# One decode step over a K and V cache: the rows of each 8 MB chunk stored in another order, and the copies' source pattern changed to match

## The chip, the cores and the metric

The kernel runs on one core of one Trainium2 chip. The metric is the device time of one execution in microseconds. The core has a matrix engine (PE, with its weight loads shown as PEld), a vector engine (DVE), a scalar engine (ACT), GpSimd (POOL) and a queue processor (SP) that here does nothing but issue transfers. Sixteen DMA engines move the data between the chip's main memory (HBM) and the core's on-chip memory (SBUF, 128 partitions).

## The reference

One token goes through one transformer block. Its attention part has 32 query heads over 8 K/V heads, with a cache of 65,536 positions of 128 numbers for each K/V head, in fp32:

```python
Hq, Hkv, Sk, Dh = 32, 8, 65536, 128
q = (x @ wq).reshape(B, Sq, Hq, Dh).transpose(0, 2, 1, 3)
k = jnp.repeat(k_cache, rep, axis=1)
v = jnp.repeat(v_cache, rep, axis=1)
scores = jnp.einsum("bhqd,bhkd->bhqk", q, k) * (Dh ** -0.5)
p = _softmax(scores, axis=-1)
o = jnp.einsum("bhqk,bhkd->bhqd", p, v)
...
h = x + _A_ref(_layernorm(x, axis=-1), A_k_cache, A_v_cache, A_wq, A_wo)
h2 = h + _B_ref(_layernorm(h, axis=-1), B_w_gate, B_w_up, B_w_down)
```

`_B_ref` is a gated feed-forward part of width 1792 with no nonlinearity: `((x @ w_gate) * (x @ w_up)) @ w_down`. There is one query row, so every number of the two caches is used once for each of four query heads, and the caches are nearly all of the data: 2 x 8 x 65,536 x 128 x 4 bytes = 536.9 MB.

## The kernel before, in words

The host cuts the K cache and the V cache of each of the 8 heads into 4 chunks. A chunk is 16,384 positions, laid out as 128 rows of 16,384 fp32 numbers, that is 128 rows of 64 KB, 8.39 MB together. For each head the 4 K chunks come first and the 4 V chunks after them, so there are 64 chunks, stored one after the other in one HBM tensor `kvd` (line 500 on). Row p of a chunk goes to partition p of the on-chip buffer.

There are two such buffers, `kv[0]` and `kv[1]` (line 62), each of the size of a chunk. SP issues the transfers of all large inputs in one order. First comes the query weight `wq` into `kv[1]` (line 118). Then the chunks follow, the even ones into `kv[0]` by `even` (line 113) and the odd ones into `kv[1]` by `odd` (line 116). Each is one copy of 128 rows. Behind the chunks come the output weight `wo`, the gate and up weights `gu` and the down weight `wd`, cut into pieces along the columns (line 149). Before each chunk but the first, SP waits for one count of the semaphore `free` (lines 139 to 144, the wait itself is in the helper `take`, line 104): that count is given when PE has finished reading the buffer into which the next transfer goes. So up to two transfers are on their way at a time, and the next one is issued when a buffer has been used.

PE reads a chunk in 32 windows of 512 columns (`windows`, line 353; the trace shows 64 matmuls per chunk; each has 32 columns of weights, and four in a row use the four quarters of the columns of the array). It waits for the chunk's semaphore before the first window (line 350): the semaphore counts 16 per copy, so all rows of a copy must have landed. For a K chunk the result is the scores of 16,384 positions, which ACT copies out of PSUM (line 217) and DVE reduces to a maximum (line 239). After four K chunks the maximum is joined over the partitions (lines 402 to 404), ACT makes the exponentials (line 221), PE transposes them (line 409), DVE writes them into the weight tile `st` (line 258), and the V chunks are multiplied by them. DVE adds the partial results (lines 269 to 274).

After the last head the output projection, the second layer norm and the feed-forward part run on the pieces of `wo`, `gu` and `wd`, and a 48 KB result goes out (line 477).

The change touches only the lines 113 and 116 and the host's expression for `kv` at line 504. The matmuls, the waits, the semaphores, the order of the issues and the content of the buffers `kv[0]` and `kv[1]` after a copy are the same.

Of the kernel before, what the change touches and what calls it, by code (L numbers as in the profile page):

```python
# [8 lines left out]
P = 128  # L9
D = 512  # L10
HKV, REP, DH = 8, 4, 128
SK = 65536
CK = 16384
NT = SK // CK
# [27 lines left out]
def body(nc, xr, kvd, wq, wo, gu, wd, out):  # L42
    pe_e, dve_e, act_e, pool_e, sp = nc.tensor, nc.vector, nc.scalar, nc.gpsimd, nc.sync

    def tile(name, *shape, align=32):
        return nc.alloc_sbuf_tensor(name, list(shape), F32, align_bytes=align).ap()
# [15 lines left out]
    kv = [tile(f"kv{i}", P, CK, align=1024) for i in range(2)]  # L62
# [22 lines left out]
    def sem(name):  # L85
        sems.append(nc.alloc_semaphore(name))
        return sems[-1]
# [7 lines left out]
    s_a0, s_a4, s_a24 = (sem(f"s_a{i}") for i in (0, 4, 24))  # L95
    s_b0, s_b20, s_b28 = (sem(f"s_b{i}") for i in (0, 20, 28))
# [13 lines left out]
        take(dve_e, own)  # L110

    def even(g):
        sp.dma_start(kv[0], kvd[g]).then_inc(s_a0, 16)

    def odd(g):
        sp.dma_start(kv[1], kvd[g]).then_inc(s_b0, 16)

    sp.dma_start(kv[1], wq).then_inc(s_b0, 16)
    pe_e.br("pe_main")
# [16 lines left out]
    pool_e.br("fin")  # L136

    even(0)
    with nc.Fori(1, end - 1, 2, engines=SP_ONLY) as c:
        for i, put in enumerate((odd, even)):  # L140
            take(sp, free)
            put(c + i)
    take(sp, free)
    odd(end - 1)

    def pieces(cuts, shift, buf, src, marks):
# [371 lines left out]
```

## Time and profile before

| | |
|---|---|
| median of 3 runs | 1308.97 us (1308.73 to 1309.02) |
| profiled execution, its own time | 1308.38 us |
| span of that execution in the trace | 1307.1 us |
| busy: PE, PEld, DVE, ACT, POOL | 676.0, 189.1, 101.6, 54.9, 4.7 us |
| moved by DMA in the span | 564.71 MB, 432 GB/s |
| time of the packets on the large queue | 99.8% of 16 engines' span |

The span runs from the first to the last instruction. Busy times leave out the issuing of transfers, branches and semaphores. A packet is one piece of a transfer as one DMA engine moves it; for a chunk a packet is one 64 KB row. The view of the transfers in a window splits the window into 40 equal slices and credits a packet's bytes to the slice in which it ends. "DMA to landing" is the time from a transfer's issue to its last byte. In the lists of groups the columns are line, engine, operation, output and input tiles, shapes, count, then busy time and mean duration, then idle time ahead of the group and what ended it.

### The profile page before, as it was taken

Reading aid. Unit: us, or ns where it says so; the run is one execution under the profiler, and the core shown is the slowest. Engines: PE = TensorE matmul, PEld = TensorE weight load, DVE = VectorE, ACT = ScalarE, POOL = GpSimd, SP = SyncE. Lnnn points to the kernel's source line nnn. Section 1 sums busy time; section 2 is a strip of 40 time slices with the busy share of each in tenths; the row PEclk is TensorE's granted clock in tenths of the full one; section 3 lists DMA queues with packets and bytes.
Section 4 is the critical chain, followed back from the end, with each engine's and each line's share of the span. In section 5 each row is a group of like instructions: output and inputs, shape, how many; then the busy total and the mean of one; then the engine's idle time right before and its main releaser. Section 6 shows DMA issues by size and latency. Waiting matters only on the chain. (4 is left out here: it accounts for less than half of the span.)

```text
span 1307.1 us, 10762 instructions
## 1 busy us (share of the span) xinstructions
PE 676.0 (52%) x4600; PEld 189.1 (14%) x4600; DVE 101.6 (8%) x250; ACT 54.9 (4%) x106; POOL 4.7 (0%) x14
## 2 busy tenths in 40 slices
PE   3446445445535545554643654454564455456458
PEld 0101111111101111111110211111111111111112
DVE  1001010010001000000100101001000100000011
ACT  0000000000000000000000000000000000000000
POOL 1000000000000000000000000000000000000000
PEclk9677677678777767767767776766776776786779
DMA  9999999999999999999999999999999999999999
GB/s 417 423 443 427 439 439 427 441 425 449 417 449 417 449 417 449 417 449 417 449 429 437 439 427 449 417 449 417 449 417 449 417 449 417 449 423 443 435 420 382
DMA packets 11154, 564.71 MB, mean 432 GB/s; under 512 B 1249, under 2 KB 1297, under 8 KB 1810
## 3 DMA queue, kind: packets, MB, share of 16 engines
q1 hardware_dynamic: 11152, 564.71, 99.8%
q10 hardware_dynamic: 2, 0.00, 0.0%
HBM read 564.66 MB, written 0.05 MB: 432 GB/s over the span
## 5 line engine op out<-in xcount | busy, mean ns | idle before, releaser
L353 PE MATMUL ps<-kv,st 128*32 128x512 f32 x4304 | 614.2, 734 | 562.7 <-DMA kv<-in_kv 542.9
L353 PEld LDWEIGHTS ps<-kv,st 128*32 128x32 f32 x4304 | 148.6, 132 | 1013.0 <-DMA kv<-in_kv 587.3
L239 DVE TENSOR_REDUCE mx<-sc 128x1 f32<-128x512 f32 x32 | 21.9, 686 | 578.9 <-DVEq L104 578.9
L409 PE MATMUL ptp<-ident,ex 128*128 128x128 f32 x128 | 28.2, 383 | 19.8 <-ACT ex L221 19.5
L217 ACT COPY sc<-ps 128x512 f32<-128x512 f32 x32 | 18.8, 586 | 438.3 <-ACTq L104 438.2
L221 ACT ACTIVATE ex<-sc,nbias 128x512 f32<-128x512 f32 x32 | 22.9, 715 | 305.9 <-ACTq L104 305.9
L271 DVE TENSOR_TENSOR orow<-ps,orow 128x512 f32<-128x512 f32 x16 | 11.1, 692 | 262.6 <-DVEq L104 262.6
L217 ACT ACT_TABLE_LOAD x8 | 10.3, 1283 | 429.0 <-ACTq L104 429.0
L258 DVE COPY st<-ptp 128x512 f32<-128x512 f32 x32 | 22.1, 692 | 45.3 <-DVEq L104 45.3
L409 PEld LDWEIGHTS ptp<-ident,ex 128*128 128x128 f32 x128 | 21.4, 196 | 22.4 <-ACT ex L221 22.3
L402 PE MATMUL sm<-ident,m 128*1 128x128 f32 x16 | 4.6, 289 | 28.3 <-DVE m L241 18.7
L274 DVE TENSOR_TENSOR orow<-ps,orow 128x256 f32<-128x256 f32 x16 | 6.1, 420 | 136.8 <-DVEq L104 136.8
L269 DVE COPY orow<-ps 128x512 f32<-128x512 f32 x8 | 5.5, 692 | 98.5 <-DVEq L104 98.5
L404 PE MATMUL sm<-ones,mexp 1*128 1x1 f32 x32 | 6.9, 281 | 6.8 <-DVE mexp L248 6.8
L440 PE MATMUL ptp<-ident,orow 128*128 128x128 f32 x32 | 6.6, 293 | 3.0 <-DVE orow L274 3.0
L402 PEld LDWEIGHTS sm<-ident,m 128*1 128x1 f32 x16 | 1.3, 79 | 42.9 <-DVE m L241 26.0
L404 PEld LDWEIGHTS sm<-ones,mexp 1*128 1x128 f32 x32 | 5.5, 213 | 9.5 <-DVE mexp L248 8.6
L221 ACT ACTIVATION_READ_ACCUMULATOR ex<-sc,nbias 128x1 f32 x32 | 6.0, 188 | 0.0
L231 DVE COPY st<-qx 128x1024 f32<-128x1024 f32 x8 | 5.6, 694 | 1.2
L373 PE MATMUL junk<-sc,mean_m 128*128 128x512 f32 x10 | 5.1, 619 | 0.0
L345 PE MATMUL ps<-ident,xn_row 1*128 1x1 f32 x4 | 0.6, 246 | 7.5 <-DVE xn_row L176 7.5
L201 DVE COPY gu_sb<-ps 128x256 f32<-128x256 f32 x4 | 1.5, 420 | 33.9 <-DVEq L104 33.9
(80 smaller groups left out, 62.9 us busy)
## 6 DMA issues: line engine op xcount, KB each, us to landing
kv<-in_wo SPq DMA_DIRECT2D x1, 5120.0 KB, 23.5
kv<-in_gu SPq DMA_DIRECT2D x1, 4096.0 KB, 20.2
kv<-in_wo SPq DMA_DIRECT2D x1, 2048.0 KB, 27.9
kv<-in_gu SPq DMA_DIRECT2D x1, 2048.0 KB, 24.6
kv<-in_wd SPq DMA_DIRECT2D x2, 1024.0 KB, 16.0
kv<-in_kv SPq DMA_DIRECT2D x64, 29.1
kv<-in_wo SPq DMA_DIRECT2D x1, 1024.0 KB, 11.8
kv<-in_gu SPq DMA_DIRECT2D x1, 1024.0 KB, 26.6
```

The source lines that it names most:

```text
L217: act_e.copy(sc[s], ps[s % 2]).then_inc(ad, 1)
L221: act_e.activation(ex[s - n], sc[s], AF.Exp, bias=nbias[:, 0:1], scale=SCALE, accum_out=sums[:, s:s + 1]).then_inc(atok[s - n], 1)
L231: dve_e.tensor_copy(st, qx.rearrange("p (g c) -> p g c", c=32)).then_inc(qt, 2)
L239: dve_e.tensor_reduce(out=mx[:, s:s + 1], in_=sc[s], axis=AX.X, op=ALU.max).then_inc(own, 1)
L258: dve_e.tensor_copy(st[:, :, 0:16].rearrange("p g (b h) -> p b g h", h=REP), ptp[n % 2].rearrange("p (b g h) -> p b g h", b=4, h=REP)).the ...
L271: mine(dve_e.tensor_tensor(out=orow, in0=ps[n % 2], in1=orow, op=ALU.add))
L274: dve_e.tensor_tensor(out=orow[:, cs], in0=ps[1][:, cs], in1=orow[:, cs], op=ALU.add).then_inc(tob, 1)
L353: i = mm(ps[buf][32 * j:32 * j + 32, :], st[:, 8 * j + r, :], kv[buf][:, w * 512:(w + 1) * 512], start=(r == 0), stop=(r in (1, 7)), skip_ ...
L402: pe_e.transpose(sm[1][0:1, 0:P], m1, ident).then_inc(pd, 1)
L404: mm(sm[0][:, 0:1], mexp.rearrange("p g h -> p (g h)"), ones[0:1, 0:1], start=True, stop=True).then_inc(pd, 1)
L409: i = pe_e.transpose(ptp[half][:, b * P:(b + 1) * P], ex[half][:, b * P:(b + 1) * P], ident)
L440: i = pe_e.transpose(ptp[1][:, b * P:(b + 1) * P], orow[:, b * P:(b + 1) * P], ident)
```

## The change

The host stores the 128 rows of each chunk in another order. The rows are seen as 16 groups of 8 (old row 8e + s, e from 0 to 15, s from 0 to 7), and are stored as 8 groups of 16, so that new row 16s + e holds old row 8e + s. The copy's source pattern undoes this: it walks e outermost (16 steps of one row, 64 KB), then s (8 steps of 16 rows, 1 MB), then the 16,384 numbers of the row. The destination pattern is unchanged: 128 partitions, one row each. So partition 8e + s receives the same numbers as before, from another address.

```diff
     def even(g):
-        sp.dma_start(kv[0], kvd[g]).then_inc(s_a0, 16)
+        sp.dma_start(kv[0], kvd[g].rearrange("(s e) x -> e s x", e=16)).then_inc(s_a0, 16)
 
     def odd(g):
-        sp.dma_start(kv[1], kvd[g]).then_inc(s_b0, 16)
+        sp.dma_start(kv[1], kvd[g].rearrange("(s e) x -> e s x", e=16)).then_inc(s_b0, 16)
...
         "kv": np.concatenate([
             lay(A_k_cache, HKV, NT, P, TPC, DH, perm=(0, 1, 4, 3, 2)).reshape(HKV, NT, P, CK),
             lay(A_v_cache, HKV, NT, P, CK),
-        ], axis=1).reshape(2 * HKV * NT, P, CK),
+        ], axis=1).reshape(2 * HKV * NT, 16, 8, CK).transpose(0, 2, 1, 3).reshape(2 * HKV * NT, P, CK),
```

The transfers of `wq`, `wo`, `gu`, `wd`, of the input row and of the result are not touched.

## The prediction

> **What bounds the kernel now.** I read the page from the top: span, busy shares, transfers.
>
> ```profile
> span 1307.1 us, 10762 instructions
> ## 1 busy us (share of the span) xinstructions
> PE 676.0 (52%) x4600; PEld 189.1 (14%) x4600; DVE 101.6 (8%) x250; ACT 54.9 (4%) x106; POOL 4.7 (0%) x14
> ...
> DMA packets 11154, 564.71 MB, mean 432 GB/s; under 512 B 1249, under 2 KB 1297, under 8 KB 1810
> ## 3 DMA queue, kind: packets, MB, share of 16 engines
> q1 hardware_dynamic: 11152, 564.71, 99.8%
> ...
> L353 PE MATMUL ps<-kv,st 128*32 128x512 f32 x4304 | 614.2, 734 | 562.7 <-DMA kv<-in_kv 542.9
> ```
>
> No compute engine is busy for more than 52% of the span, while the packets of the large queue fill 99.8% of what sixteen DMA engines have. PE's main group stands idle for 562.7 us, 542.9 of them waiting for chunks. The kernel is bound by its transfers from end to end.
>
> How even is that stream? Next I read the groups of the two lines that issue chunks, for the spacing of the issues, and the windows by stretch.
>
> ```profile
> L113 SPq DMA_DIRECT2D kv<-in_kv x32: 332/333/422, 1.2 to 1210.1; - x32
> ...
> DMA to landing us min/median/max: 28.2/29.1/40.8
> ```
>
> ```profile
> L116 SPq DMA_DIRECT2D kv<-in_kv x32: 332/333/343, 32.1 to 1229.9; - x32
> ```
>
> ```profile
> core 0: us, PE busy (x) PEld busy (x) DVE busy (x) ACT busy (x) POOL busy (x), PEclk, DMA share, GB/s
> 0.00:20.00 20.00, 0.58 (x4) 0.50 (x4) 4.56 (x16) 1.58 (x2) 4.68 (x14) 1.00 1.00 420
> 20.00:40.00 20.00, 11.73 (x76) 3.68 (x76) 1.95 (x6) 0.00 (x0) 0.00 (x0) 0.92 0.97 419
> 100.00:1200.00 1100.00, 568.43 (x3855) 158.51 (x3855) 82.19 (x189) 48.81 (x96) 0.00 (x0) 0.73 1.00 434
> ```
>
> The 32 issues of the odd chunks lie between 32.1 and 1229.9 us, so 31 intervals of two chunks take 1197.8 us, or **19.32 us per chunk**. A chunk is 128 rows of 65,536 bytes, so this is 434.2 GB/s, the 434 of the long window. If each engine takes 8 of the 128 rows, a row takes 19.32 / 8 = **2.415 us** and one engine moves 27.1 GB/s. A transfer lands 29.1 us after its issue (median) though its own moving takes 19.32, so it waits 9.8 us behind its predecessor; the queue is never empty.
>
> The last view is the one that I rest the forecast on: the transfers between 600 and 620 us, in slices of 0.5 us.
>
> ```profile
> DMA  0009000690009900099000990009600090006900
> GB/s 0 0 0 2097 0 0 0 262 1835 0 0 0 786 1311 0 0 0 1180 918 0 0 0 1442 655 0 0 0 1835 262 0 0 0 2097 0 0 0 262 1835 0 0
> DMA packets 144, 8.39 MB, mean 419 GB/s; under 512 B 16, under 2 KB 16, under 8 KB 16
> ```
>
> A slice at 2097 GB/s holds 1.05 MB, which is 16 rows. Rows end in bursts of 16, within one slice or two neighbouring ones, and then nothing ends for about 2 us. So **the sixteen engines go in step**, all at the same 27.1 GB/s, and they still do so after thirty chunks: neither the compute beside them nor the chunk makes one of them late. Had HBM been the limit I would expect engines to get ahead of one another; a rate this rigid looks like a fixed limit that each engine meets alone.
>
> **The change, part by part.** It adds and removes no instruction; a chunk stays 128 rows of 64 KB. What moves is which address each row has, and which engine carries which row to which partitions.
>
> (a) *Issue.* The source pattern has one more dimension. An issue takes 333 ns now; the slowest copy that SP issues, 422 ns, bounds what a longer pattern might add by 0.1 us, and I allow as much again. Below nothing it can't matter either: the 9.8 us that a transfer waits behind its predecessor hide it. Without that cover it would be 64 x 0.1 = 6 us. I take 0.
>
> (b) *Reading neighbours.* The gain that it could bring is bounded by the rows. In the steady stretch a row takes 2.415 us whatever else happens. The poorest stretches are the first two windows, 420 and 419 GB/s against 434. All of the shortfall there is (434 - 419.5) / 434 x 40 us = 1.3 us, and only the part after `wq` has changed addresses. I take 0, with -1.3 as the end on this side. For a loss through the reading order the nearest row is the same: 3.3% slower over the whole stream is 0.033 x 1236 = +41 us.
>
> (c) *Writing.* This is where I choose. The source's outermost dimension becomes 16, the destination's stays 128 partitions. If a copy is dealt out by outermost index, engine e now gets source group e. By the order in which both patterns are walked that is partitions 8e to 8e + 7, one after another. Before, both sides counted 128, and the trace doesn't show which 8 partitions one engine had. Suppose that data enters SBUF through sixteen entrances, each serving a fixed group of partitions at no more than the 27.1 GB/s that one engine moves. Today's even rate then says that today's deal puts one engine on each entrance. A deal in neighbouring eights need not. If two engines in step write to one entrance and half of the entrances stand idle meanwhile, each row takes two row times, 4.83 us. They don't part again by themselves, since the burst view shows that engines keep step. The ends are 0 (a deal that collides nowhere) and one more row time per row (every row collides with one other): 64 chunks x 8 rows x 2.415 us = **+1236.5 us**. I take the upper end, less what the engines' small stagger saves. A pair that is apart by t collides t less in each half of a chunk. The bursts lie within one or two slices, so t is 0.5 us at most, and the pair that is closest together sets the landing; with 0.1 us it is 128 x 0.1 = 13 us.
>
> [...] The trace agrees with sixteen engines per copy: 78 copies on the large queue make 1248 of the 1249 packets under 512 B. [...]
>
> (d) *What is late next.* PE waits longer: a chunk then comes each 38.6 us, and PE's idle time grows by about the 1236 us. A buffer is free again some 10 us after its chunk landed, as now, and the next issue still falls into the transfer of the other buffer, so the queue stays full. The tail is unchanged:
>
> ```profile
> 1283.89 17.78 DMA kv<-in_wd
> ```
>
> **The sum.** The profiled execution took 1308.4 us (span 1307.1 and 1.3 around it), 0.6 under the median of 1309.0. 1308.4 + 1236.5 - 13 = **2532 us**.
>
> **The rivals.**
>
> *Nothing changes* (the other side). The limit of 27.1 GB/s sits in the DMA engine itself, or the rows go to the engines as before, so that the change doesn't do what it says or does it without effect. For it: the rigid rate, which an engine's own limit explains as well; reading order can't matter to such an engine. Against it: it needs a place without an entrance limit, or a deal that doesn't collide. It decides as soon as no two engines share an entrance in the same row time. Time: 1308.4 + 0 to + 2, say 1309 us.
>
> [...]
>
> *Rows are read more slowly.* One engine's successive rows now lie 1 MB apart rather than 64 KB. If the reading of rows at that distance, by engines that keep step, meets in the same part of HBM, each per cent longer row costs 0.01 x 1236.5 = 12.4 us. With the nearest row's 3.3% it is 1350 us. For it: the engines' common step. Against: at any moment the sixteen engines would read one stretch of 1 MB. [...] No run here shows a large pitch.
>
> *Faster.* Neighbouring rows help the first chunks and shave the row time. The 1.3 us of (b) are within noise; a gain over 0.2% needs rows under 2.41 us in the whole stream: 1305 us.
>
> **How the numbers follow.** Collisions in step 55%, out of step 16%, slower reading 6%, nothing 20%, faster 3%. So slower by over 0.2% has 77%, within 0.2% (2.6 us, about what a measurement of this kernel can tell from no change) 20%, faster 3%. The likeliest time is 2532 us, its own range 2480 to 2550. The cases below it can't be left out, since leaving out no change and faster alone would be 23%; so the range is 1307 to 2560, and 3% (faster) and a few per cent above remain outside.
>
> **What would show it.** Right: the issues of line 116 are 77 us apart instead of 38.6, the long window shows 217 GB/s while the queue's share of packets stays near 100%, bursts of 16 rows come 4.83 us apart, and from the `wo` pieces on the rate is back at about 430. Out of step: rows of two lengths, bursts broken up. Slower reading: all rows longer by one ratio that isn't two. Wrong: an issue spacing of 38.6 us and unchanged bursts. Then (c) failed, and the limit was the engines' own or the deal didn't collide.

## The result, and the profile after

The changed kernel takes 2659.9 us (median of 6 runs, 2655.9 to 2669.2) against 1308.9 us before: a ratio of **2.034, 95% interval 2.031 to 2.036**. The profiled execution has a span of 2667.8 us.

The page of the changed kernel, in the same order as for the kernel before:

```profile
span 2667.8 us, 10762 instructions
## 1 busy us (share of the span) xinstructions
PE 678.2 (25%) x4600; PEld 189.6 (7%) x4600; DVE 103.0 (4%) x250; ACT 54.9 (2%) x106; POOL 4.4 (0%) x14
...
DMA packets 11154, 564.71 MB, mean 212 GB/s; under 512 B 1249, under 2 KB 1297, under 8 KB 1810
## 3 DMA queue, kind: packets, MB, share of 16 engines
q1 hardware_dynamic: 11152, 564.71, 100.0%
...
L353 PE MATMUL ps<-kv,st 128*32 128x512 f32 x4304 | 616.3, 736 | 1919.7 <-DMA kv<-in_kv 1895.2
```

The same instructions, the same busy time on the compute engines, the same 11,154 packets and the same bytes. The DMA engines are as busy as before (100.0% of their span), at half the rate. PE's wait for chunks has grown from 542.9 to 1895.2 us, by 1352 us, which is nearly all of the 1361 us between the two profiled executions. A "busy" DMA engine is one that has a packet open; the share doesn't say that the packet moves at full speed.

The issues of the odd chunks, the windows by stretch, and the landings between 600 and 620 us in slices of 0.5 us:

```profile
L116 SPq DMA_DIRECT2D kv<-in_kv x32: 562/563/582, 33.6 to 2542.6; - x32
...
DMA to landing us min/median/max: 70.5/71.3/72.0
```

```profile
core 0: us, PE busy (x) PEld busy (x) DVE busy (x) ACT busy (x) POOL busy (x), PEclk, DMA share, GB/s
0.00:20.00 20.00, 0.58 (x4) 0.50 (x4) 6.01 (x16) 1.58 (x2) 4.39 (x14) 1.00 1.00 420
20.00:40.00 20.00, 12.79 (x76) 3.83 (x76) 1.95 (x6) 0.00 (x0) 0.00 (x0) 0.98 1.00 210
100.00:2500.00 2400.00, 592.88 (x4035) 164.19 (x4039) 83.45 (x191) 49.94 (x98) 0.00 (x0) 0.61 1.00 207
```

```profile
GB/s 0 0 0 0 0 131 1180 655 131 0 0 0 0 0 0 0 918 786 393 0 0 0 0 0 0 0 1180 524 393 0 0 0 0 0 0 0 786 918 393 0
DMA packets 64, 4.19 MB, mean 210 GB/s; under 512 B 0, under 2 KB 0, under 8 KB 0
```

The loss begins with the first chunk: while `wq` moves (0 to 20 us) the rate is 420 GB/s as before, in the next window it is 210. The issues give (2542.6 - 33.6) / 62 = 40.47 us per chunk, **5.06 us per row** on average where it was 2.415. Sixteen rows still end together: a burst fills three or four slices, some 1.5 us, then nothing ends until the next, about 5.1 us after the last. The trace also keeps each packet's own start and duration, and these packet records say the same: about three of four 64 KB rows take 5.1 us and one of four 4.9, where nearly all took 2.42 before. (The 5.12 us and the 6% in the expectations below are of the longer rows alone; over all rows it is 5.06 us and 5%.) No engine gets ahead, and the view at 2500 us looks the same.

### The profile page after: what moved, and what is told of

Same layout as the page of the kernel before. It is cut to its first block, busy times and chain, and to the rows that moved or that the text cites. A ratio compares the mean times of both kernels' runs of the same rounds, so it can differ in the third digit from the quotient of the medians.

```text
span 2667.8 us, 10762 instructions
## 1 busy us (share of the span) xinstructions
PE 678.2 (25%) x4600; PEld 189.6 (7%) x4600; DVE 103.0 (4%) x250; ACT 54.9 (2%) x106; POOL 4.4 (0%) x14
## 2 busy tenths in 40 slices
DMA packets 11154, 564.71 MB, mean 212 GB/s; under 512 B 1249, under 2 KB 1297, under 8 KB 1810
## 5 line engine op out<-in xcount | busy, mean ns | idle before, releaser
L353 PE MATMUL ps<-kv,st 128*32 128x512 f32 x4304 | 616.3, 736 | 1919.7 <-DMA kv<-in_kv 1895.2
## 6 DMA issues: line engine op xcount, KB each, us to landing
kv<-in_kv SPq DMA_DIRECT2D x64, 71.3
```

Of the source, the lines that this page charges most:

```text
L353: i = mm(ps[buf][32 * j:32 * j + 32, :], st[:, 8 * j + r, :], kv[buf][:, w * 512:(w + 1) * 512], start=(r == 0), stop=(r in (1, 7)), skip_ ...
```

## The experiments

All of these kernels compute the full result. Each was run beside the kernel before, which took 1308.8 to 1308.9 us every time. Only the edits of the chunks' copies and of the host's layout are shown; where a chunk is split into several copies, the counts of its semaphore are raised to match.

**The deal alone, with the old addresses.** The host keeps the old order; only a gap of 4 KB is put behind each group of 8 rows, so that the source pattern keeps three dimensions.

```diff
-        sp.dma_start(kv[0], kvd[g]).then_inc(s_a0, 16)
+        sp.dma_start(kv[0], kvd[g][:, 0:8 * CK].rearrange("e (s x) -> e s x", s=8)).then_inc(s_a0, 16)
...
+    arrays["kv"] = np.pad(arrays["kv"], ((0, 0), (0, 0), (0, 1024)))
```

> Theory A (entrances): the new deal gives engine e the partitions 8e to 8e + 7, so engines in step write in pairs to one way into SBUF. Theory B (reading): the new addresses are read more slowly. This kernel keeps the old order of the rows in HBM (each group of 8 rows only lies 4 KB further from the next), and has only the new deal, by a source pattern whose outermost dimension is 16. A: as the changed kernel, a chunk each 40.5 us, about 2660 us; if the 6% by which a shared row (5.12 us) exceeds twice 2.415 us comes from the reading, then a chunk each 38.6 us and about 2545 us. B: about 1309 us.

Measured: 2658.8 us in a single run, like the changed kernel's 2659.9. The long window:

```profile
100.00:2500.00 2400.00, 598.75 (x4047) 165.75 (x4047) 84.72 (x193) 49.91 (x98) 0.00 (x0) 0.61 1.00 208
```

The rows are where they were (but for 4 KB), and the rate is that of the changed kernel. The order of the rows in HBM has no part in the loss; the form of the source pattern makes all of it, the 5% beyond the doubling included.

**The pitch alone, with the old deal.** Sixteen chunks are stored row by row through one another, so that a chunk's rows are 1 MB apart. The copies stay plain; SP's loop is written out, since the address is no longer a multiple of the loop's count.

```diff
-        sp.dma_start(kv[0], kvd[g]).then_inc(s_a0, 16)
+        sp.dma_start(kv[0], kvd[g // 16][:, g % 16, :]).then_inc(s_a0, 16)
...
-        ], axis=1).reshape(2 * HKV * NT, P, CK),
+        ], axis=1).reshape(4, 16, P, CK).transpose(0, 2, 1, 3),
```

> The old deal (128 partitions outermost on both sides, no pattern of three dimensions), but 16 chunks are stored row by row through one another, so that successive rows of a chunk lie 1 MB apart, as the rows of one engine do in the changed kernel. Theory A (entrances): no change, 1309 us within 0.2%. Theory B (reading): a good part of the changed kernel's loss of 1351 us comes back, 1350 to 2660 us.

Measured: 1322.9 us, ratio 1.0116 (1.0099 to 1.0133). Neither theory as I had put it: there is a loss, but of 14 us. The windows show where it lies:

```profile
20.00:40.00 20.00, 12.66 (x76) 3.84 (x76) 1.94 (x6) 0.00 (x0) 0.00 (x0) 0.96 0.94 367
40.00:140.00 100.00, 48.94 (x331) 13.30 (x331) 6.05 (x12) 5.14 (x9) 0.00 (x0) 0.72 1.01 411
140.00:600.00 460.00, 232.35 (x1584) 64.88 (x1588) 32.67 (x76) 19.98 (x39) 0.00 (x0) 0.73 1.00 431
600.00:1200.00 600.00, 309.49 (x2089) 84.25 (x2085) 42.78 (x97) 24.54 (x47) 0.00 (x0) 0.71 1.00 433
```

and the landings of the same kernel between 600 and 620 us, in slices of 0.5 us:

```profile
GB/s 262 524 918 393 0 262 786 786 262 131 131 918 655 262 262 0 1049 655 131 262 131 1180 393 131 262 393 1049 262 131 262 262 1049 524 0 262 393 1049 393 0 262
```

The first chunks are slow, and then the full rate comes back. By that time the bursts are gone: rows end in nearly every slice. SP's written-out loop is not what costs: packets fill 99.7% of sixteen engines' span, against 99.8% before, and the 64 KB packets themselves take 12 us more per engine than before. The copies' destinations are the same, so the loss lies in reading. That engines meet there, and are parted by it, is argued and wasn't tested; shown is that with the engines apart the pitch costs next to nothing (433 GB/s).

**No reordering and no third dimension, but 64 partitions at a time.** And its control, two copies of half the columns.

```diff
-        sp.dma_start(kv[0], kvd[g]).then_inc(s_a0, 16)
+        for h in (0, 64):
+            sp.dma_start(kv[0][h:h + 64, :], kvd[g][h:h + 64, :]).then_inc(s_a0, 16)
```

```diff
-        sp.dma_start(kv[0], kvd[g]).then_inc(s_a0, 16)
+        for h in (0, CK // 2):
+            sp.dma_start(kv[0][:, h:h + CK // 2], kvd[g][:, h:h + CK // 2]).then_inc(s_a0, 16)
```

> The kernel before, with each chunk copied as two plain copies of 64 partitions one behind the other (0 to 63, then 64 to 127): old order of the rows, no pattern of three dimensions. [...] If a row costs more because of the changed pattern or of its addresses: about 1309 us.

> Control for the previous kernel: two copies per chunk as well, but each of all 128 partitions and half of the columns, so 32 KB rows and the old deal. Theory A: 1309 us, at most 1% more for the larger number of packets. If two copies per chunk were what costs in the previous kernel: as slow as that one.

Measured: 2666.0 us for the halves (a single run), 1311.4 us for the columns, ratio 1.002 (1.001 to 1.003). The long windows, first of the halves, then of the columns:

```profile
100.00:2500.00 2400.00, 593.83 (x4003) 166.34 (x4007) 83.60 (x191) 49.91 (x98) 0.00 (x0) 0.61 1.00 207
```

```profile
100.00:1200.00 1100.00, 569.70 (x3854) 158.23 (x3855) 81.62 (x189) 48.73 (x96) 0.00 (x0) 0.73 1.00 433
```

Plain copies in the old order run at the changed kernel's 207 GB/s as soon as sixteen engines write to 64 neighbouring partitions, and two copies per chunk as such don't matter. So the limit depends on **which partitions are written at the same time**: 207 GB/s with 64 of them, 433 with all 128.

**Fewer partitions at a time.** Eight copies of 16 partitions, and four copies of 32:

```diff
-        sp.dma_start(kv[0], kvd[g]).then_inc(s_a0, 16)
+        for h in range(0, P, 16):
+            sp.dma_start(kv[0][h:h + 16, :], kvd[g][h:h + 16, :]).then_inc(s_a0, 16)
```

> The kernel before, each chunk copied as eight plain copies of 16 neighbouring partitions, one row per engine in each. [...] Theory A: a row takes four times 2.415 us and the same 6% on top as in the shared row of two (5.12 against 4.83), 10.2 us, a chunk 82 us, together about 5320 us; 5010 if there is no such extra. If a pair is the most that can meet: 2660 us. If many small copies were only dearer to handle: below 1500 us.

> Why a shared row takes 5.12 us and not 4.83: each chunk as four plain copies of 32 neighbouring partitions, two rows per engine. [...] If sharing by two costs 6% as such: rows of 5.1 us, about 2660 us. [...]

Measured: 4855.6 us for 16 partitions, 2666.5 us for 32 (a single run each). The long windows, first with 16, then with 32 partitions:

```profile
100.00:4500.00 4400.00, 583.85 (x3968) 159.97 (x3960) 81.51 (x185) 49.67 (x95) 0.00 (x0) 0.56 1.00 112
```

```profile
100.00:2500.00 2400.00, 592.15 (x4003) 164.96 (x4007) 83.32 (x191) 49.94 (x98) 0.00 (x0) 0.61 1.00 207
```

32 partitions are no worse than 64, and 16 are worse again. Per engine this is 434 / 16 = 27.1 GB/s with 128 partitions, 207 / 16 = 12.9 with 64 or 32 and 112 / 16 = 7.0 with 16. The second is about 5% less than half of the first (13.6), the third 3% more than a quarter (6.8): by the packet records a row takes 9.34 us with 16 partitions, less than four times 2.415, and the 4855.6 us lie below both times that I had worked out for four (5010 and 5320). That two or four engines meet at one entrance was my assumption; no run shows how many entrances there are, nor which partitions share one. Why 32 partitions are as fast as 64, and why the half loses 5% and the quarter nothing, is left open.

**Taking the collision away by time.** First the ground: halves of 64 partitions, dealt in 16 groups of 4. Then the same with two small copies at the start, which only half of the engines carry.

```diff
+        for h in (0, 64):
+            sp.dma_start(kv[0][h:h + 64, :], kvd[g][h:h + 64, :].rearrange("(s e) x -> e s x", e=16)).then_inc(s_a0, 16)
...
-        ], axis=1).reshape(2 * HKV * NT, P, CK),
+        ], axis=1).reshape(4 * HKV * NT, 16, 4, CK).transpose(0, 2, 1, 3).reshape(2 * HKV * NT, P, CK),
```

```diff
+    pad = tile("pad", 64, CK // 2)
+    for h in (0, 32):
+        sp.dma_start(
+            pad[h:h + 32, :],
+            kvd[0][h:h + 32, 0:CK // 2].rearrange("(s e) x -> e s x", e=8)).then_inc(s_pad, 16)
     sp.dma_start(kv[1], wq).then_inc(s_b0, TOTAL)
```

> [...] Theory A: about 2660 us, as with the plain halves (2666).

> The previous kernel with one thing more, at the very start: two small copies of 8 groups (to a tile that nothing reads), which by the count of 8 run on eight engines only, the lower-numbered ones, and give each of them the work of four rows, 9.7 us. [...] Theory A: the collisions go; a chunk each 19.3 us again, and about 1330 us (10 us for the small copies, 10 for the first meeting of the two groups). If a row is slow because of its pattern, of the number of partitions of a copy, or of what it reads: 2660 us as before it. If engines that are apart are drawn back into step: between the two, from fast to slow in the course of the run.

Measured: 2658.9 us without the small copies (a single run); with them four runs took 1653.2, 1680.7, 1704.1 and 1715.5 us. Two copies of 1 MB at the start take 943 to 1006 us off a kernel whose 128 chunk copies are unchanged. The packets agree with eight engines for each of them: 2289 are under 512 B, 16 more than without the two copies, where a copy on all engines brings 16 by itself (78 copies made 1248 of them in the kernel before). Which eight no view shows. The landings of the kernel with the small copies (the run of 1704.1 us) between 600 and 620 us, in slices of 0.5 us, and its windows:

```profile
GB/s 1180 393 524 0 0 393 1049 655 0 0 0 1311 262 524 0 0 0 0 0 524 918 131 524 0 0 524 918 655 0 0 0 1442 262 393 0 0 655 786 524 131
```

```profile
50.00:200.00 150.00, 67.14 (x430) 19.56 (x422) 9.39 (x20) 6.67 (x13) 0.00 (x0) 0.67 1.00 352
400.00:1600.00 1200.00, 467.95 (x3181) 129.16 (x3185) 66.85 (x154) 38.45 (x74) 0.00 (x0) 0.67 1.00 331
```

The pattern, the copies' sizes, the addresses and the partitions are the same as in the slow kernel beside it; only the time at which each engine moves its rows has changed. This shows that the slow row is a meeting in time. That they meet in writing is what the slow kernels with the old addresses (2658.8 us) and the halves (2666.0 us) say, and the fast one with the neighbours' order below (1308.4 us).

The time stays 320 to 390 us over my 1330. A part of the rest is in the view: two and a half microseconds pass in which no row ends, and at 1000 us such a pause comes every 12.5 us or so, once per copy of 64 partitions. The engines don't run dry in it, though: packets fill 99.6% of sixteen engines' span. By the packet records there are rows of two lengths instead: a quarter of the 64 KB rows take some 4.4 us, and most of the others 2.7. So it looks as if one row of the four in each copy still meets. Why it does, and why the other rows take 2.7 us and not 2.42, is left open. From 400 us on the rate stays between 330 and 335 GB/s, so the engines are not drawn back into step.

**Which deals collide.** 32 groups of 4 rows outermost, once with old addresses (a gap of 4 KB behind each group), once with the neighbours' order that the change is after.

```diff
-        sp.dma_start(kv[0], kvd[g]).then_inc(s_a0, 16)
+        sp.dma_start(kv[0], kvd[g][:, 0:4 * CK].rearrange("e (s x) -> e s x", s=4)).then_inc(s_a0, 16)
```

```diff
-        sp.dma_start(kv[0], kvd[g]).then_inc(s_a0, 16)
+        sp.dma_start(kv[0], kvd[g].rearrange("(s e) x -> e s x", e=32)).then_inc(s_a0, 16)
...
-        ], axis=1).reshape(2 * HKV * NT, P, CK),
+        ], axis=1).reshape(2 * HKV * NT, 32, 4, CK).transpose(0, 2, 1, 3).reshape(2 * HKV * NT, P, CK),
```

> As the kernel with the new deal only, but with 32 groups of 4 rows outermost instead of 16 groups of 8 (each group 4 KB further from the next). If the deal goes straight along the outermost index whenever the two sides count differently, engine e has the groups 2e and 2e + 1, again partitions 8e to 8e + 7: about 2660 us. If only the count of 16 spoils the old deal, and groups of 4 partitions can still be dealt as before: about 1309 us.

> The idea of the change with the deal that didn't collide: 32 groups of 4 rows outermost, and the host's order made to fit (new row 32s + e holds old row 4e + s), so that at any moment the sixteen engines read rows out of one stretch of 32 neighbours. Theory A, with reading that is not the limit: 1309 us within 0.2%. If neighbouring rows are read faster: below 1306 us. If engines' own rows 2 MB apart are read more slowly, as in the kernel with a pitch of 1 MB: some 1310 to 1325 us.

Measured: 1308.6 us (a single run) with the old addresses; 1308.4 us with the neighbours' order, ratio 0.9998 (0.9989 to 1.0007). The issues of the odd chunks and the long window of the second:

```profile
L116 SPq DMA_DIRECT2D kv<-in_kv x32: 555/556/574, 31.7 to 1231.4; - x32
```

```profile
100.00:1200.00 1100.00, 569.81 (x3855) 159.05 (x3855) 82.09 (x189) 48.73 (x96) 0.00 (x0) 0.73 1.00 434
```

A source pattern of three dimensions is not what costs, nor is a count that differs between the two sides: 32 groups of 4 run as fast as the plain copy. Sixteen groups of 8 don't. A deal straight along the outermost index would have given engine e the partitions 8e to 8e + 7 with 32 groups as well, so it is not the general rule. And with the collision gone, reading neighbouring rows is worth nothing that these runs can show. The idea of the change, tried by itself, is neutral; its form is what doubled the time.

## Why the prediction was right or wrong

**The bound and the reading order (b): right for this change.** Reading neighbours doesn't move the even 2.415 us per row: without collision it gives a ratio of 0.9998, and my end of -1.3 us was never reached. That reading can cost something all the same is shown by the pitch of 1 MB with the old deal, 14 us.

**The deal and the entrances (c): a meeting in writing was right, its size was off.** The runs show that the rate goes by which partitions are written at the same moment: 434 GB/s with 128 of them, 207 with 64 or 32, 112 with 16. The sixteen entrances, each for a fixed group of partitions, were my supposition; no run shows them, nor which two engines meet, and that every row collides with one other was a choice that nothing before the result had shown. Named for this were issues 77 us apart, a rate of 217 GB/s at a share near 100%, bursts 4.83 us apart. Measured were 81 us (2 x 40.47), 207 GB/s at 100.0%, and about 5.1 us. The term that failed is "one more row time per row", 2.415 us, which I took for the upper end of what a meeting of two can cost. The runs showed 5.06 - 2.415 = 2.65 us in its place. The trace of before holds no shared row, so two halves of 27.1 GB/s were an assumption, not a bound; with 64 or 32 partitions two engines together pass 25.9 (2 x 207 / 16). Why they pass less is open.

From there to the measured time: 64 chunks x (40.47 - 38.64) = 117 us for the shared row, 13 us that I had subtracted for the stagger and that have to go back in, since the measured 40.47 already holds what the stagger saves, and some 7 us at both ends of the stream: 2532 + 117 + 13 + 7 = 2669 us, the profiled execution (2667.8 and 1.3 around it). The 7 us are that execution's own, as (d) shows; without them it is 2662 us, against the median of 2659.9. The range ended at 2560 for the same reason; it should have left room above a doubling. The 13 us were worked out from a pair that meets anew in each half of a chunk; no run shows that, and what the runs show in its place is the 40.47 us per chunk.

The way to the mechanism was in part lucky. "If a copy is dealt out by outermost index" fits the rate of 16 groups of 8, but not that of 32 groups of 4; had the change used 32 groups, the same reasoning would have forecast a doubling that does not come.

**Issue (a):** right in effect, low in price. The issue went from 333 to 563 ns, a little more than the 0.2 us that I allowed; behind the queue's cover it costs nothing, as the 556 ns of the kernel with 32 groups show, which takes 1308.4 us.

**What is late next (d): right for PE; the sign in the tail missed in the profiled execution.** PE waits, and nothing else moves. Its wait grew by 1352 us and not by 1236, for the reason of (c). A buffer is free some 10 us after its chunk has landed, as forecast (80.9 us from issue to issue, 71.3 to landing). But from the `wo` pieces on the rate should have been back at about 430 GB/s, and the tail unchanged. Before and after:

```profile
1262.00:1280.00 18.00, 14.22 (x102) 3.83 (x98) 1.92 (x7) 0.00 (x0) 0.00 (x0) 0.81 1.00 430
```

```profile
2625.00:2660.00 35.00, 25.68 (x164) 7.80 (x164) 3.85 (x20) 0.00 (x0) 0.00 (x0) 0.85 0.99 370
2639.33 22.97 DMA kv<-in_wd
```

The last stretch of the chain of waits is 22.97 us where it was 17.78; this is most of the 7 us above. It doesn't come with the new deal: the kernel with the deal alone moves 430 GB/s between 2609 and 2651 us. Why the last pieces were slow in the profiled execution is open.

**The rivals.** *Nothing changes* fell, though its idea of an engine's own limit isn't refuted: with 16 partitions four engines together move 28.0 GB/s (4 x 112 / 16). If it is four that meet at one place, which was not shown, that place passes more than 27.1, and the 27.1 of a single engine may be its own. *Out of step* did not happen by itself: step is kept over 2600 us, and it took two more copies at the start to part the engines. *Rows are read more slowly* fell for this kernel, where the old addresses are as slow, but it is real elsewhere: at 1 MB from row to row of a chunk the window from 20 to 40 us fell to 367 GB/s. Over the whole run this pitch cost 14 us, most of it in the first half.

## What to carry to other kernels

When a stream runs at the same rate in every slice with all DMA engines in step, ask first which partitions the engines write at the same moment, and not how they read: a copy with all 128 partitions outermost (or 32 groups of 4) ran at 434 GB/s, one with 16 groups of 8, or of 64 or 32 partitions only, at 207. A reshape of a source pattern that leaves bytes, packets and busy shares as they were can still change who writes where, so look at the rate and at the spacing of landings; the busy share of the DMA engines is 99.8% before and 100.0% after. And a resource that the trace has never shown shared has no upper end in "twice" (here a row went from 2.415 to 5.06 us): leave room above it.

## What the runs showed that was not expected

With 64 or 32 partitions at a time two engines move less together (25.9 GB/s) than one alone with all 128 (27.1), and with 16 partitions four move more (28.0). A loss in reading and a collision in writing behave differently: with rows 1 MB apart the engines come apart and the rate recovers from 367 to 433 GB/s, while the sixteen engines of the changed kernel stay together to the last chunk, at 207 GB/s from 100 to 2500 us. And 32 groups of 4 rows keep the full rate (434 GB/s) where 16 groups of 8 halve it (207). How a copy is dealt to engines can't be read from these traces directly; it is inferred from the rates.
